# Five of seven opening groups of unread matmuls left out of a delta-rule and Fourier-mixing kernel

## The chip, the cores and the metric

One core of one Trainium2 chip. The metric is the device time of one execution in microseconds (us). 649.44 us is the median of three runs of the kernel before (649.12 to 649.47).

## The reference

The kernel joins an attention block with a recurrent state (the delta rule) and a Fourier mixing block with an MLP. There are 4 batches, 8 heads, 768 positions and 48 channels per head; the model width is 8 x 48 = 384.

```
k_n = k / (norm(k) + 1e-6)
for t in range(768):
    y[t]  = q[t] @ state
    v_old = state^T @ k_n[t]
    state = state + beta[t] * outer(k_n[t], v[t] - v_old)
x = y as (batch, seq, 384)
u = x + real(fft(fft(x, axis=seq), axis=channels))
un = layer-normalised u
out = u + relu(un @ w_ch1) @ w_ch2
```

## The kernel before

The sequence of a batch is cut into blocks of 128 positions; one batch and one block of all 8 heads is a unit, 24 units in all. Units are worked on in rounds: the first of four units, the second of two, and six of three. Within a unit, the recurrence over 64 positions is turned into matrix form, so that a small triangular matrix has to be inverted for each head; the rest are matmuls. The Fourier transforms are matmuls with tables, and the MLP is two matmuls with weights that come as 64-bit floats and are converted on the chip.

**The order of all work is planned ahead.** The class Plan (lines 74 to 394) takes operations with their dependencies, engines and estimated durations; `schedule` (line 190) simulates the engines with a list scheduler and writes down one order over all engines in `self.order`; `issue` (line 387) then walks through that order and emits the instructions, engine by engine in that order. `pace` (line 374) ties a load that SP issues after 6 us of planned time to the last computing operation that the plan has ended by then, so loads follow the computation.

**Unread matmuls.** The planner has a model of the clock of TensorE, and where TensorE would have nothing to do in some stretches, it puts in operations of its own, with the number -1 (lines 273 to 285). What they emit is in `idle` (lines 2256 to 2272). If the planned time is under E2 = 5.0 us, a group is six matmuls of 128 rows and 64 columns on the zeroed tile pb (line 2263); the profile shows two records for each, so 12 matmul records and 12 weight loads. Later groups are one or two matmuls of 256 columns (line 2270), on pb first and on the table pack later. Nobody reads their results: they go to a free PSUM bank. E0 = 1.0 us is the planned time from which groups are put in. Each group is planned as 0.432 us long at full clock.

**How the kernel opens.** SP issues the loads of k for the first six units (tile us, `load`, line 670, by `dma`, line 613, whose instructions have line 615), then q and v. ScalarE's queue loads pack (the identity and masks) and beta. VectorE and GpSimd zero tiles, pb among them. TensorE's order is: seven groups on pb (line 2263), the transposes of unit 0's k (`turn`, line 688; instructions at line 571), the transposes of beta (line 2078), two groups of line 2270, then transposes of the next unit and key products of the one before it (`keys`, line 709; instructions at line 568) in turn, up to the sixth unit. Then come 16 groups of two matmuls (line 2270, 64 records in the profile), the transposes and products of the q of the first units, and 14 groups more (56 records). VectorE and ScalarE copy each transposition out of PSUM (lines 577 and 579) and collect the key products in the tile gd (lines 577 and 748). VectorE turns gd round (line 902), inverts the small triangular matrices column by column (lines 928 to 968, tiles w and tmp) and turns the result back (line 986); TensorE's first products of the next stage read that.

```
for i in range(6):
    I(nc.tensor.matmul(pst[two[0]][0:64, 64 * i:64 * i + 64], lhsT=w[:, 0:64],
                       rhs=w[:, 64:128], start=True, stop=True,
                       skip_group_check=True))
```

Of the kernel before, what the change touches and what calls it, by code (L numbers as in the profile page):

```python
# [38 lines left out]
WIN, WARM, COLD, CLOCK = 3.413, 600.0, 560.0, True  # L39
LOOK, EARLY = 1e9, 19.0271  # L40
FOLD, BY, SEQ, HOT, HOTPE, HOTPK, HOTG, NORM = 1, 1, 1, 1.7459, 0, 0, 0, 1
HOTC, PORT, E2 = 1, 1, 5.0
GAP, HALF = 0.3228, 84.0008
LATE = -8.0806
PLOOK, PHOLD, PEND = 28.9494, 0.4978, 115.7679
# [28 lines left out]
class Plan:  # L74
# [312 lines left out]
    def issue(self):  # L387
        at = {}
        for o in self.order:
            self.ins = None  # L390
            o.fn(o.eng)
            at[id(o)] = self.ins
            if o.after is not None:
                self.tc.add_manual_dep(self.ins, at[id(o.after)].name, mybir.DependencyInfo(
                    mybir.DependencyClass.Sync, mybir.DependencyReason.DATA), reason="pace")
# [1913 lines left out]
```

## Time and profile before

| | |
|---|---|
| median of three runs | 649.44 us |
| the profiled execution | 648.84 us |
| its span, first to last instruction | 647.0 us |
| mean granted TensorE clock | 0.995 |
| instructions | 22,705 |

The profile is of one execution. Lines such as L568 are lines of the kernel; many instructions have the line of a helper (568 matmul, 571 transposition, 577 and 579 copies by ScalarE and VectorE, 615 loads). PE is TensorE's matmul and PEld its weight load, DVE is VectorE, ACT ScalarE, POOL GpSimd, SP SyncE. "out<-in" names the tiles. A row of the chain of waits has start, length and what; a row of the timeline has start, length, engine, line, operation and count, and in brackets the idle time before and who ended it. A matmul's record includes its latency, so records overlap and a busy TensorE is not one at its peak.

### The profile page before, as it was taken

The numbers are of one execution on the slowest core, as the hardware profiler recorded it, in microseconds if no ns is written. First come the engines' busy times: TensorE is split into PE (matmuls) and PEld (weight loads), VectorE is DVE, ScalarE is ACT, GpSimd is POOL, SyncE is SP. The second block draws the span as 40 slices with busy tenths as digits, with TensorE's granted clock in tenths as the row PEclk, the third lists the DMA queues.
The fourth block names the chain that finished last, engine by engine and source line by source line (L and its number), as shares of the span: only waits on it lengthen the run. The fifth ranks groups of instructions, "written<-read, shape, count | busy, mean of one in ns | idle before, by whom it ended". The sixth has DMA issues, their size and how long they took to land.

```text
span 647.0 us, 22705 instructions
## 1 busy us (share of the span) xinstructions
PE 632.9 (98%) x9748; PEld 516.6 (80%) x9748; DVE 507.3 (78%) x1529; ACT 271.6 (42%) x804; POOL 39.8 (6%) x44
## 2 busy tenths in 40 slices
PE   9998899999999999999999999999999999999998
PEld 8788788777777877877777777877777699899997
DVE  4998779999997379999863899999828633976573
ACT  3769665543154544421655333345442113321120
POOL 4103313230000000000000000000000000000000
PEclk9999889999999999999999999999999999999999
DMA  6654534550013231000323220000000000000000
GB/s 126 142 161 134 123 100 110 135 152 2 25 28 87 54 64 27 25 1 2 71 46 64 52 51 2 23 5 3 3 27 3 2 24 1 26 2 25 2 25 24
DMA packets 82808, 31.98 MB, mean 49 GB/s; under 512 B 75667, under 2 KB 79732, under 8 KB 82580
## 3 DMA queue, kind: packets, MB, share of 16 engines
q1 hardware_dynamic: 82516, 30.31, 19.3%
q8 instruction: 76, 1.25, 0.8%
q10 hardware_dynamic: 192, 0.23, 0.2%
q14 instruction: 24, 0.20, 0.1%
HBM read 25.81 MB, written 4.72 MB: 47 GB/s over the span
## 4 chain that ended last, share of the span: by engine, by line
PE 77%; DVE 15%; ACT 4%; issue 2%; DMA 1%; DVEq 0%; ACTq 0%
PE pp L568 72%; PE pp L571 3%; DVE rr L1056 2%; DVE tmp L1051 2%; PE pp L2270 1%; PE pp L2263 1%; ACT us L577 1%; DMA ws<-in_moe_w_ch_dram 1%; DVE gd L812 1%; DVE w L968 1%; ACT w L2017 1%; DVE tmp L962 1%; DVE R L1453 1%; DVE rr L902 1%; DVE w L2036 1%
## 5 line engine op out<-in xcount | busy, mean ns | idle before, releaser
L568 PE MATMUL pp<-R,w 128*128 128x256 f32 (+1 forms) x832 | 182.2, 367 | 0.7 <-DVE us L789 0.7
L568 PEld LDWEIGHTS pp<-R,w 128*128 128x128 f32 x832 | 145.6, 190 | 20.2 <-DVE us L789 0.9
L568 PE MATMUL pp<-w,R 128*128 128x384 f32 x384 | 134.6, 495 | 0.0
L577 ACT ACTIVATE us<-pp 32x128 f32<-32x128 f32 (+3 forms) x232 | 73.1, 348 | 87.4 <-PE pp L568 65.2
L568 PEld LDWEIGHTS pp<-w,R 128*128 128x128 f32 x384 | 70.2, 190 | 41.3
L1697 ACT ACTIVATE R<-pp 128x512 f32<-128x512 f32 x47 | 28.1, 597 | 102.3 <-PE pp L568 92.8
L568 PE MATMUL pp<-us 64*64 64x64 f32 (+4 forms) x2784 | 67.1, 231 | 0.0
L568 PEld LDWEIGHTS pp<-us 64*64 64x64 f32 (+2 forms) x2784 | 56.9, 132 | 5.8 <-issue 3.2
L1056 DVE TENSOR_TENSOR rr<-rr,tmp 128x84 f32<-128x84 f32 (+13 forms) x180 | 57.7, 335 | 1.5
L1051 DVE TENSOR_TENSOR tmp<-rr 128x84 f32<-128x84 f32 (+14 forms) x180 | 57.2, 332 | 1.4
L577 ACT ACTIVATE R<-pp 128x192 f32<-128x192 f32 (+8 forms) x103 | 29.7, 332 | 29.5 <-PE pp L568 18.4
L568 PEld LDWEIGHTS pp<-u,us 64*64 64x64 f32 (+2 forms) x1248 | 29.0, 129 | 15.6 <-issue 10.2
L577 ACT ACTIVATE x<-pp 64x192 f32<-64x192 f32 x91 | 28.3, 323 | 27.4 <-PE pp L568 24.0
L1362 DVE TENSOR_TENSOR u<-u,pp 64x192 f32<-64x192 f32 x66 | 22.1, 349 | 18.8 <-PE pp L568 14.5
L1391 DVE TENSOR_TENSOR st<-st,pp 128x192 f32<-128x192 f32 x30 | 10.5, 351 | 33.5 <-PE pp L568 30.4
L1872 DVE TENSOR_TENSOR us<-us,pp 128x256 f32<-128x256 f32 x64 | 26.8, 420 | 12.3 <-ACT us L577 10.8
L2270 PE MATMUL pp<-pack 64*64 64x256 f32 (+1 forms) x198 | 35.0, 396 | 0.1
L568 PE MATMUL pp<-u,us 64*64 64x48 f32 (+3 forms) x1248 | 34.5, 217 | 0.0
L568 PE MATMUL pp<-st,us 48*64 48x48 f32 (+2 forms) x1184 | 29.5, 223 | 2.6 <-issue 1.1
L568 PEld LDWEIGHTS pp<-st,us 48*64 48x64 f32 (+2 forms) x1184 | 25.0, 135 | 8.3 <-issue 4.9
L1828 DVE TENSOR_TENSOR gd<-us 128x128 f32<-128x128 f32 x48 | 11.8, 289 | 21.8 <-ACT us L1904 15.4
L568 PE MATMUL pp<-us,gd 128*128 128x192 f32 x144 | 27.8, 327 | 0.0
(176 smaller groups left out, 999.6 us busy)
## 6 DMA issues: line engine op xcount, KB each, us to landing
out_dram<-x SPq DMA_DIRECT2D x11, 384.0 KB
us<-in_k_dram SPq DMA_DIRECT2D x16, 192.0 KB
us<-in_q_dram SPq DMA_DIRECT2D x16, 192.0 KB
us<-in_v_dram SPq DMA_DIRECT2D x16, 192.0 KB
us<-in_k_dram SPq DMA_DIRECT2D x8, 181.5 KB
us<-in_q_dram SPq DMA_DIRECT2D x8, 181.5 KB
us<-in_v_dram SPq DMA_DIRECT2D x8, 181.5 KB
x<-in_moe_w_ch_dram SPq DMA_DIRECT2D x3, 484.0 KB
```

What stands on the lines that cost most here:

```text
L568: I(nc.tensor.matmul(o, lhsT=lhsT, rhs=rhs, start=start, stop=stop, skip_group_check=True))
L571: I(nc.tensor.matmul(o, lhsT=src, rhs=ident[p0:p0 + n, p0:p0 + n], is_transpose=True, start=start, stop=True, skip_group_check=True))
L577: I(nc.scalar.activation(o, i, ACT.Copy, **({} if scale is None else {"scale": scale})))
L812: I(nc.vector.scalar_tensor_tensor(w[0], w[1], (m1, m0)[s], w[2], op0=ALU.mult, op1=ALU.add))
L1051: I(eng(e).tensor_tensor(T_, R[:, :, j + 1:32, j:j + 1].broadcast_to([128, ns, n, j]), R[:, :, j:j + 1, 0:j].broadcast_to([128, ns, n, j]) ...
L1056: I(eng(e).tensor_tensor(R[:, :, j + 1:32, 0:j], R[:, :, j + 1:32, 0:j], T_, op=ALU.add))
L1362: I(nc.vector.tensor_tensor(U[:, s], U[:, s], psum(b1[s])[a, s0:s1].rearrange("p (j d) -> p j d", d=D), op=ALU.subtract))
L1391: I(nc.vector.tensor_tensor(sn[:, s0:s1], so[:, s0:s1], psum(b2)[:, s0:s1], op=ALU.add))
L1697: I(nc.scalar.activation(o, s, ACT.Relu))
L1828: vec(128, lambda e, j=j, i0=i0, i1=i1, op=op: I(nc.vector.tensor_tensor(s(j), i0, i1, op=op)), [aH] + rd, [aS(j)], pr - P.ev)
L1872: vec(256, lambda e: I(nc.vector.tensor_tensor(o, i0(), i1(), op=ALU.add)), [], [aH] + list(wr), pr - P.ev, use=n)
L2270: I(nc.tensor.matmul(pst[two[0]][x, 0:256], lhsT=w[x, 0:n], rhs=w[x, 0:256], start=True, stop=True, skip_group_check=True))
```

## The change

`issue` skips the planner's own operations whose planned start lies from 2.5 to 5.4 us. The plan is made as before and its order is the same, so all other instructions follow each other on each engine as they did. Of the seven groups of six matmuls that open TensorE's program the first two stay and the last five are gone: 30 calls, 60 matmul records and 60 weight loads.

```diff
-HOTC, PORT, E2 = 1, 1, 5.0
+HOTC, PORT, E2, E3 = 1, 1, 5.0, 2.5
...
     def issue(self):
         at = {}
         for o in self.order:
+            if o.i < 0 and E3 <= o.start < E2 + 0.4:
+                continue
             self.ins = None
             o.fn(o.eng)
```

## The prediction

> **What bounds the kernel now.** I read the page first, for the engine that carries the end and for the first chain, then the chain of waits over the first 37 us, then the instructions of TensorE in order of time, then windows and DMA at the places that the change touches.
>
> ```profile
> span 647.0 us, 22705 instructions
> ...
> PE 632.9 (98%) x9748; PEld 516.6 (80%) x9748; DVE 507.3 (78%) x1529; ACT 271.6 (42%) x804; POOL 39.8 (6%) x44
> ...
> PE 77%; DVE 15%; ACT 4%; issue 2%; DMA 1%; DVEq 0%; ACTq 0%
> ```
>
> TensorE has work in nearly all of the span, but 98% says little here: much of the early work is matmuls that nobody reads. The chain (start, length, what) tells which stretch counts:
>
> ```profile
> 1.18 7.20 PE pp L2263 x84
> 8.38 0.39 PE pp L571 x8
> ...
> 13.76 0.62 PE pp L568 x32
> ...
> 14.83 0.45 ACT gd L577
> ...
> 16.62 1.96 DVE rr L902
> ...
> 24.84 0.33 DVE us L579
> ...
> 35.90 0.98 DVE gd L986
> 36.88 0.14 issue
> 37.01 4.90 PE pp L568 x160
> ```
>
> The reader is to see three legs: 84 unread matmuls (42 calls, two records each; seven groups of 12), then the transposes and key products of six units to about 14.4, then VectorE's inversion to 36.9, where TensorE takes over. Whatever moves the first leg moves all that follows, if TensorE keeps pace beside VectorE. The second condition is in TensorE's own order of time:
>
> ```profile
> 8.31 0.46 PE L571 MATMUL pp<-pack,us 64*128 64x64 f32 x8
> 8.70 0.56 PE L2078 MATMUL pp<-pack,x 32*128 32x32 f32 x6
> 9.19 1.13 PE L2270 MATMUL pp<-pb 128*128 128x256 f32 x4
> 10.25 0.46 PE L571 MATMUL pp<-pack,us 64*128 64x64 f32 x8
> 10.64 0.69 PE L568 MATMUL pp<-us 48*64 48x64 f32 x32
> ...
> 14.71 0.70 PE L2270 MATMUL pp<-pack 128*128 128x256 f32 x2
> 15.34 1.16 PE L568 MATMUL pp<-us 48*64 48x64 f32 x64
> 16.32 7.08 PE L2270 MATMUL pp<-pack 64*64 64x256 f32 x64
> 23.33 0.96 PE L571 MATMUL pp<-pack,us 64*128 64x64 f32 x24
> ...
> 30.58 6.21 PE L2270 MATMUL pp<-pack 64*64 64x256 f32 x56
> 37.01 2.08 PE L568 MATMUL pp<-gd,w 64*64 64x64 f32 x64 [0.22 <-DVE gd L986]
> ```
>
> Two more runs of unread matmuls (L2270, 7.0 and 6.2 us) stand in TensorE's order and block it while they last; the second ends at 36.79, only 0.22 us before VectorE's result. So at 37 us **two chains arrive together**, VectorE's and TensorE's, and TensorE has a slack of 0.22 us.
>
> **What the change removes.** Five groups of 12: 60 matmuls and their 60 weight loads. Their price is not one number, because the pace changes inside the stretch:
>
> ```profile
> 1.18:5.80 4.62, 4.62 (x43) 1.00 0.94 193
> 5.80:8.40 2.60, 2.60 (x46) 1.00 1.05 208
> ```
>
> Columns: window, length, PE busy (instructions), granted clock, DMA. The same instruction is issued each 4.62/43 = 0.107 us up to 5.8, and then the other 41 in 2.51 us, each 0.061 us. The clock cell says 1.00 in both, so it can't be trusted here: I read the pace as a slow clock up to 5.8. The two groups kept are 24 x 0.107 = 2.57 us and end at 1.18 + 2.57 = 3.75. The five removed are 19 at 0.107 and 41 at 0.061, 4.5 us.
>
> **What is late next.** TensorE's first read instruction needs the pack table and the first k load. Packets that had gone by 3.55 and by 4.3 us:
>
> ```profile
> q1 hardware_dynamic: 1035, 0.20, 27.2%
> ...
> q1 hardware_dynamic: 1965, 0.37, 42.6%
> ```
>
> A k load is 8 heads x 128 rows = 1024 lines of 192 bytes. If the loads go in order, the first is in by 3.6; if two share the engines, by 4.3; and the semaphore instruction ahead of the transposes bounds it from above:
>
> ```profile
> L571 PEldq EVENT_SEMAPHORE  x1: 51/51/51, 7.2 to 7.2; - x1
> ```
>
> It passes at 7.2, whether it had to wait or only stood in the queue. I take **4.35**: the packets are nearer to that than to 7.2. At 930 packets in 0.75 us the other units follow each 0.8 us, earlier than TensorE asks for them. The transposes then start 8.31 - 4.35 = 3.96 us earlier. That is the most that can be won. No wait is added, but this one becomes visible, with all of TensorE's order behind it.
>
> SP's loads from 12 us on go along with it, since they wait for what was computed, so a shift does not meet a fixed DMA time:
>
> ```profile
> SPq L615 <- ACT us L577: 5.2, 4, 1.5
> SPq L615 <- DVE us L579: 5.2, 1, 5.2
> ```
>
> **What the five groups did for the clock.** This is the term that decides. The only other place where the trace shows the clock go down and up again (same columns, with PEld, DVE, ACT and POOL between):
>
> ```profile
> 67.25:70.67 3.42, 2.83 (x59) 2.25 (x57) 3.33 (x9) 2.81 (x10) 0.00 (x0) 1.00 0.56 111
> 70.67:74.08 3.41, 3.41 (x98) 3.12 (x96) 2.08 (x7) 2.38 (x8) 2.61 (x2) 1.00 0.69 167
> 74.08:77.49 3.41, 1.80 (x66) 1.54 (x64) 3.33 (x9) 1.41 (x4) 0.21 (x1) 1.00 0.71 207
> 77.49:80.91 3.42, 3.42 (x59) 3.15 (x58) 1.72 (x5) 2.15 (x6) 3.42 (x2) 0.50 0.37 70
> 80.91:84.32 3.41, 3.41 (x31) 2.60 (x28) 0.65 (x2) 2.08 (x7) 0.49 (x1) 0.50 0.47 93
> ```
>
> The clock is set in steps of 3.41 us. It fell after a step with 1.80 us of work, and one whole step with TensorE busy for 3.42 of 3.42 did not bring it back: only the second did. The records include their latency, so by streaming time (the columns of each matmul at 0.107 us for 64) I make the failing step about 94% (some 0.2 us between its shapes) and the one that worked 95% or more. Before the change the groups fill one step without a gap (2.40 to 5.81, on the same grid of 3.41 us), and the clock came at 5.8. After it the groups fill 2.57 us, then come 0.6 us of nothing, then transposes and products with a change of shape each half a microsecond. One unit's pair (L571 x8, L568 x32) takes 1.02 us, of which 12 issues x 0.061 are 0.73: 0.145 us goes at each change. So the best step there is filled to about 88%. I take it that **the clock stays low** until a long run fills a step: the 64 L2270 matmuls.
>
> [...]
>
> **The sum with a low clock.** A row gives four 64-row products of 128 columns:
>
> ```profile
> 78.02 1.98 PE L568 MATMUL pp<-us 48*64 48x128 f32 x32
> 79.78 0.95 PE L568 MATMUL pp<-st,us 64*64 64x64 f32 x13
> ```
>
> 1.76 us for 8 fours, so 0.11 us for a four of 64 columns. Then, with 0.145 us for each change:
> - a transposition: 4 pairs x 0.107 + 0.145 = 0.57 (0.39 before); a key product: 8 x 0.11 + 0.145 = 1.02 (0.63 before); the pair 1.6 instead of 1.02;
> - L2078: between 0.49 (as now) and 0.98 (doubled); I take 0.75;
> - the four L2270: 1.06 now, of which some 0.2 for changes; the rest doubled, 1.9.
>
> From 4.35: 4.92, 5.67, 7.57 after the first transposition, L2078 and L2270; then 0.57 + 1.02 for the first two, and three pairs: 9.16 + 4.8 = 13.96 for the fourth unit's product, which ended at 14.38. VectorE's chain starts **0.4 us earlier**. TensorE goes on: a transposition 0.57, two L2270 1.06, 16 fours 1.9: 17.5 instead of 16.32, **1.2 us later**. Now the 64 L2270 start at the low clock, 0.22 instead of 0.11 us each. A step must lie wholly in them or the fours just before (from 15.6 to 17.5), and where the steps lie in another execution is open, so the clock comes between 19.0 and 24.3; I take the middle, 21.6. The run ends at 21.6 + 7.0 - (21.6 - 17.5)/2 = 26.55, where it ended at 23.33: 3.2 us later (1.9 to 4.6).
>
> From there TensorE's work up to 36.79 is the same at full clock. VectorE has a copy of those late transposes in its order (L579 at 24.84), so it loses its 0.4 us there and waits some 2 us too. At 37.01 the end is TensorE's: 3.2 - 0.22 = 3.0 later. One stall of TensorE's weight loads lies between, and may take part of it back:
>
> ```profile
> PEld pp L568 <- issue: 0.6, 1, 0.6
> ```
>
> With 0.5 of that I take **+2.5 us**, with ends +1.2 and +4.0. After 37 us each stage waits for the one before it and all keep the shift.
>
> **Code loading** I cost at nothing, with both ends open:
>
> ```profile
> PEld pp L568 <- issue: 21.8, 54, 1.2
> ...
> q8 instruction: 76, 1.25, 0.8%
> ```
>
> 76 loads for 2 x 9748 instructions are one for each 256; 120 fewer moves each by half a block. The 54 stalls that may be theirs have a mean of 0.4 us and a longest of 1.2, so a shift could give or take about 1 us.
>
> The profiled execution took 648.84 us (span 647.0 and 1.84 around it), 0.60 below the median 649.44. 648.84 + 2.5 = 651.34; with 0.60 put back, **651.9 us**. A measurement of this kernel tells about 0.2% (1.3 us) from no change.
>
> **Rivals.**
> - **Early clock** (the other side, faster). The point that decides: does one step with TensorE busy to about 88% lift the clock? For it: the groups' step did with one. Against it: the step at 77.49. It would come between 7.8 and 11.2, say 9.5, after the first product; the other three pairs run at 1.02 us and the fourth product ends at about 12.4 instead of 14.38. TensorE and VectorE are both 2.0 us earlier (1.4 to 2.5): 647.4. The ceiling, if the clock were high from 4.35 on, is 3.96 us: 645.5.
> - **Clock after two busy steps**, as at 77.49. It comes near 12.6; the fourth product ends near 13.5, TensorE's leg 0.7 earlier: -0.8, 648.6, within what can be told from no change.
> - **Not what it says**: the first k load is later than I read, near 7.2, and TensorE waits in place of the groups. Then up to 1.1 us are won at the start and the clock lost all the same: between 649 and 653.
>
> **Chances.** Low clock into the long run 0.52 (0.49 of it above +1.3 us); early clock 0.27; two steps 0.13 (0.03 of it below -1.3); the rest, late load or code loading, 0.08, spread over all. Faster by over 0.2%: 0.27 + 0.03 + 0.03 = 0.33; slower: 0.49 + 0.02 = 0.51; within: 0.16. The likeliest case alone spans 650.6 to 653.5. The range takes in most of the early clock: **647.0 to 653.5**.
>
> **What would show it.** TensorE's L2263 row: x24 from 1.18, ending near 3.75. L571's first start: 4.3 to 4.4 if the first load is as read; later means the load. L571 and L568 between 5 and 14 us: pairs each 1.6 us are a low clock, 1.02 a high one. The first run of 64 L2270: an end at 25 to 28 bears me out, one before 22 the early clock. VectorE's L902: near 16.2. L568 on gd at 37.01: 39 to 40 against 35. I am wrong if that last row starts before 37, or if it is late and the end of the span is not.

## The result and the profile after

The kernel after takes **653.08 us** (median of 20 runs, 648.98 to 660.51), the one before 649.23 us on the same chips (20 runs, 647.12 to 652.01). Medians in this document are of all runs; the ratios leave out a run more than 1.5% above its kernel's fastest (660.51 here, and one run each of e1_refill and e9_tab_pieces). The ratio after to before is **1.0063**, with a 95% interval of 1.0042 to 1.0084: 4.1 us slower (2.7 to 5.5). The forecast was 651.9 us in 647.0 to 653.5. Lines of the kernel after are two higher: L570 is what L568 was, L573 was L571, L2265 was L2263, L2272 was L2270.

The page of the kernel after (its profiled execution took 653.18 us):

```profile
span 651.4 us, 22585 instructions
...
PE 632.7 (97%) x9688; PEld 514.5 (79%) x9688; DVE 507.4 (78%) x1529; ACT 271.6 (42%) x804; POOL 39.8 (6%) x44
...
PE 81%; DVE 13%; ACT 3%; issue 3%; DMA 1%; DVEq 0%; ACTq 0%
```

The 60 matmuls are gone (9748 to 9688), and the span is 4.4 us longer. The opening is not where this comes from. TensorE in order of time:

```profile
1.18 2.82 PE L2265 MATMUL pp<-pb 128*64 128x64 f32 x24 [1.18 <-DVE pb L695]
...
4.12 0.46 PE L573 MATMUL pp<-pack,us 64*128 64x64 f32 x8
...
6.06 0.46 PE L573 MATMUL pp<-pack,us 64*128 64x64 f32 x8
...
7.08 0.46 PE L573 MATMUL pp<-pack,us 64*128 64x64 f32 x8
...
32.83 2.08 PE L570 MATMUL pp<-gd,w 64*64 64x64 f32 x64 [0.21 <-DVE gd L988]
```

The transposes start at 4.12 where they started at 8.31; the next two are 1.02 us apart, the pace of a high clock; and the products on gd start at 32.83 instead of 37.01. In this execution the opening gained 4.2 us. An instruction that runs 30 times between 196 and 503 us, VectorE's update of the state, is a ruler for the rest (count, shortest/median/longest ns, first and last start). First before, then after:

```profile
L1391 DVE TENSOR_TENSOR st<-st,pp x30: 333/354/355, 196.5 to 503.0; 128x192 f32<-128x192 f32 x30
```

```profile
L1393 DVE TENSOR_TENSOR st<-st,pp x30: 340/354/355, 196.6 to 507.3; 128x192 f32<-128x192 f32 x30
```

Of the 4.2 us won by 37 us nothing is left at 196 (+0.1), and 4.2 more are lost by 507. The chain of waits shows the first loss:

```profile
42.73 4.36 PE pp L570 x171
47.10 1.79 issue
48.89 2.80 PE pp L570 x91
...
52.88 2.48 issue
55.36 7.74 PE pp L570 x179
```

TensorE stands still twice, for 1.79 and 2.48 us, with no engine that releases it. The window from one restart up to the next stall (columns as in the prediction):

```profile
48.88:52.95 4.07, 3.99 (x128) 3.56 (x128) 2.89 (x9) 3.37 (x12) 0.15 (x1) 1.00 0.81 291
```

128 matmuls and 128 weight loads stand between the two stalls: 256 instructions, the size that the prediction had worked out for one load of code. The queue that loads code moved nothing from 51.75 to 53, then one block of code between 53.0 and 54.2, and TensorE started again at 55.36, 1.2 us after that window. The row of the code queue in it (packets, MB, share):

```profile
q8 instruction: 1, 0.02, 5.0%
```

TensorE's idle times by who ended them (sum, count, longest), before and after:

```profile
PE pp L568 <- issue: 1.5, 2, 1.1
```

```profile
PE pp L570 <- issue: 7.1, 5, 2.5
...
PEld pp L570 <- issue: 29.6, 63, 2.6
```

The weight loads' longest was 1.2 us before. Behind two of the three long stalls the granted clock is 0.50 for a step of 3.41 us. Around the third, 1.66 us that end at 214.86, two steps of the clock in the kernel after, with the step behind the second stall as a third row, and then the same stretch as the first two before the change:

```profile
212.17:215.59 3.42, 1.76 (x81) 1.47 (x68) 0.70 (x2) 1.61 (x6) 0.00 (x0) 1.00 0.30 58
215.59:219.00 3.41, 3.41 (x7) 1.74 (x6) 0.00 (x0) 1.43 (x6) 0.00 (x0) 0.50 0.04 7
...
55.16:58.58 3.42, 3.22 (x48) 2.88 (x48) 1.07 (x5) 1.58 (x5) 3.40 (x3) 0.50 0.02 5
```

```profile
212.10:215.51 3.41, 3.41 (x89) 2.49 (x76) 0.70 (x2) 3.06 (x11) 0.00 (x0) 1.00 0.33 65
215.51:218.92 3.41, 3.41 (x149) 2.74 (x148) 2.07 (x7) 1.28 (x5) 0.00 (x0) 1.00 0.34 67
```

After the step with 1.76 us of work the granted clock is 0.50 for the next one, as it is behind the stall that ends at 55.36; before the change it stays at 1.00 around 215. The price can be read off the eight matmuls that follow (pp<-w,R, 384 columns): 4.54 us instead of 2.85. With the 1.66 us of the stall that is 3.35 of the 4.2 us lost between the ruler's ends.

### The profile page after: what moved, and what is told of

It reads as the page before. It is cut to its first block, busy times and chain, and to the rows that moved or that the text cites. A ratio compares the mean times of both kernels' runs of the same rounds, so it can differ in the third digit from the quotient of the medians.

```text
span 651.4 us, 22585 instructions
## 1 busy us (share of the span) xinstructions
PE 632.7 (97%) x9688; PEld 514.5 (79%) x9688; DVE 507.4 (78%) x1529; ACT 271.6 (42%) x804; POOL 39.8 (6%) x44
## 4 chain that ended last, share of the span: by engine, by line
PE 81%; DVE 13%; ACT 3%; issue 3%; DMA 1%; DVEq 0%; ACTq 0%
PE pp L570 75%; PE pp L573 3%; DVE rr L1058 2%; DVE tmp L1053 2%; PE pp L2272 2%; DMA us<-in_q_dram 1%; DVE gd L814 1%; DVE w L970 1%; DVE tmp L964 1%; DVE rr L904 1%; ACT x L579 1%; DVE rr L860 0%; ACT us L579 0%; PE pp L2265 0%; ACT w L2019 0%
## 5 line engine op out<-in xcount | busy, mean ns | idle before, releaser
L570 PE MATMUL pp<-R,w 128*128 128x256 f32 (+1 forms) x832 | 183.9, 370 | 0.7 <-DVE us L791 0.7
L570 PEld LDWEIGHTS pp<-R,w 128*128 128x128 f32 x832 | 146.8, 192 | 20.8 <-DVE us L791 0.9
L570 PE MATMUL pp<-w,R 128*128 128x384 f32 x384 | 136.3, 500 | 0.0
L570 PEld LDWEIGHTS pp<-w,R 128*128 128x128 f32 x384 | 70.9, 192 | 42.2 <-issue 1.7
L570 PE MATMUL pp<-us 64*64 64x64 f32 (+4 forms) x2784 | 67.5, 230 | 6.4 <-issue 6.4
L570 PEld LDWEIGHTS pp<-us 64*64 64x64 f32 (+2 forms) x2784 | 56.9, 132 | 12.6 <-issue 10.1
L570 PEld LDWEIGHTS pp<-u,us 64*64 64x64 f32 (+2 forms) x1248 | 29.6, 130 | 15.7 <-issue 10.2
L570 PE MATMUL pp<-u,us 64*64 64x48 f32 (+3 forms) x1248 | 35.3, 219 | 0.0
L2272 PE MATMUL pp<-pack 64*64 64x256 f32 (+1 forms) x198 | 34.8, 395 | 0.1
L570 PE MATMUL pp<-st,us 48*64 48x48 f32 (+2 forms) x1184 | 29.0, 222 | 1.8 <-DVE st L1393 0.7
L570 PEld LDWEIGHTS pp<-st,us 48*64 48x64 f32 (+2 forms) x1184 | 24.4, 134 | 7.6 <-issue 3.7
L570 PE MATMUL pp<-us,gd 128*128 128x192 f32 x144 | 27.8, 327 | 0.0
```

The source lines that it names most:

```text
L570: I(nc.tensor.matmul(o, lhsT=lhsT, rhs=rhs, start=start, stop=stop, skip_group_check=True))
L2272: I(nc.tensor.matmul(pst[two[0]][x, 0:256], lhsT=w[x, 0:n], rhs=w[x, 0:256], start=True, stop=True, skip_group_check=True))
```

## Theories and experiments

**Theory A**: TensorE's code is loaded in blocks of 256 instructions (an estimate: 2 x 9748 instructions for the 76 loads of the kernel before) that end at fixed counts of its stream. Leaving out 120 instructions moves every block end onto other work, and where the new ends fall into short matmuls the load comes too late. **Theory B**, the forecast: in most executions the clock stays low in the opening, and that is the loss. **Theory C**, formed after the first three runs: executions come in two kinds, by whether the groups kept lift the clock at once or not.

### Put the instructions back without work: e1_refill

On the kernel after, the unread matmuls of the first long run are issued in halves, so that 120 instructions come back with no more columns. The block ends beyond 26 us lie on the same work as before the change.

```diff
-                I(nc.tensor.matmul(pst[two[0]][x, 0:256], lhsT=w[x, 0:n], rhs=w[x, 0:256],
+                for c in ((0, 128), (128, 256)) if mode == "64" and 13.5 < now < 20.0 else ((0, 256),):
+                    I(nc.tensor.matmul(pst[two[0]][x, c[0]:c[1]], lhsT=w[x, 0:n], rhs=w[x, c[0]:c[1]],
```

> The changed kernel with 120 instructions put back later: 15 of the 16 groups in the first long run of unread matmuls (L2270 in the kernel before) are issued as halves of 128 columns, so that TensorE streams the same columns in the same time but its code blocks of 256 instructions end from there on where they ended before the change. Theory A (the code blocks have moved, and their late loads stop TensorE behind 40 us): the 4 us won in the opening stay, 645 to 647 us, and the stalls of 2.0 and 2.7 us near 47 and 53 us are gone. Theory B (low clock in the opening of most executions, as forecast): no better than the changed kernel, 652 to 654.

646.23 us against 649.22, ratio 0.9969 (0.9944 to 0.9995). The ruler and the waits:

```profile
L1393 DVE TENSOR_TENSOR st<-st,pp x30: 327/353/355, 193.1 to 499.3; 128x192 f32<-128x192 f32 x30
```

```profile
PE pp L570 <- issue: 0.8, 1, 0.8
...
PEld pp L570 <- issue: 21.1, 53, 1.0
```

The opening's gain is now kept to the end (-3.4 at 193, -3.7 at 499), and the long stalls are gone. So with its block ends put back the same removal is not slower but **faster**, though its interval only just excludes no change: A. The intervals of this kernel and of the kernel after (1.0042 to 1.0084) lie well apart.

### Move the block ends alone: e2_shift_only

On the kernel before, the seven opening groups do the same columns in 12 matmuls instead of 42: 120 instructions fewer, meant to take TensorE the same time.

```diff
-                for i in range(6):
-                    I(nc.tensor.matmul(pst[two[0]][0:64, 64 * i:64 * i + 64], lhsT=w[:, 0:64],
-                                       rhs=w[:, 64:128], start=True, stop=True,
+                for i in range(2 if now < 4.4 else 1):
+                    m = 256 if now < 4.8 else 128
+                    I(nc.tensor.matmul(pst[two[0]][0:64, 0:m], lhsT=w[:, 0:64],
+                                       rhs=w[:, 0:m], start=True, stop=True,
```

> The kernel before with its seven opening groups issued as 12 matmuls of up to 256 columns in place of 42 of 64: TensorE streams unread columns up to about 8.4 us as before, but with 120 instructions fewer, so the code blocks stand as in the changed kernel. Theory A: the loss without the gain, stalls of 2 us and more near 51 and 57 us, 653 to 658. Theory B: as before, 649 to 650.

653.92 us against 649.22, ratio 1.0082 (1.0054 to 1.0109). TensorE in order of time, and the ruler:

```profile
1.18 8.14 PE L2264 MATMUL pp<-pb 128*64 128x256 f32 x24 [1.18 <-DVE pb L693]
9.26 0.46 PE L571 MATMUL pp<-pack,us 64*128 64x64 f32 x8
...
54.28 0.40 PE L568 MATMUL pp<-us 64*64 64x64 f32 x12 [2.04 <-issue]
```

```profile
L1391 DVE TENSOR_TENSOR st<-st,pp x30: 335/353/356, 198.1 to 509.7; 128x192 f32<-128x192 f32 x30
```

It is not a pure shift: the transposes start 0.95 us late (9.26 against 8.31). Beyond that, the stall stands before the same 12 matmuls as in the kernel after, and from 198 to 510 us it loses 5.1 us (+1.6, then +6.7). Counted in the traces, 1113 matmuls start before the restart at 54.28, and 1113 before the one at 48.89 in the kernel after; the later stalls, too, stand at the same counts in both (3661, 5824 and 7988). In the kernel before, where the count 1113 falls on other work, TensorE waits 0.35 us there.

### The change once more: e3_again

The kernel after, unaltered, for another execution's profile.

> The changed kernel once more, for a second look at its opening. Theory A: first products of the next stage (tile gd, 37.01 us before) near 33 us in this execution too, stalls at 47 and 53 us, 652 to 654. Theory B: the clock comes later than 8 us and those products start after 37 us.

653.63 us against 649.22, ratio 1.0082 (1.0054 to 1.011). This profiled execution (656.88 us) opened in the other way:

```profile
4.23 0.69 PE L573 MATMUL pp<-pack,us 64*128 64x64 f32 x8 [0.23 <-DMA us<-in_k_dram]
...
7.64 0.69 PE L573 MATMUL pp<-pack,us 64*128 64x64 f32 x8
...
9.31 0.69 PE L573 MATMUL pp<-pack,us 64*128 64x64 f32 x8
...
17.89 8.28 PE L2272 MATMUL pp<-pack 64*64 64x256 f32 x64
...
39.39 2.08 PE L570 MATMUL pp<-gd,w 64*64 64x64 f32 x64
```

A transposition takes 0.69 us instead of 0.46, a pair 1.67 instead of 1.02. The run of 64 takes 8.28 instead of 7.08 us, so some 11 of its matmuls ran at the low clock (1.20 us at 0.11 each), and the clock came about 2.4 us into it, at 20.3. The products on gd start 2.4 us late. This is the forecast's opening, and it shows what didn't lift the clock here: three steps in a row with TensorE busy throughout in the records (the last three rows). The first row shows where the steps lie here: one ends at 3.24, behind 19 of the 24 matmuls kept.

```profile
3.24:6.66 3.42, 3.19 (x25) 2.67 (x24) 1.01 (x18) 0.38 (x1) 3.42 (x4) 1.00 1.12 230
6.66:10.07 3.41, 3.41 (x55) 2.41 (x57) 0.90 (x5) 0.39 (x1) 1.74 (x3) 1.00 0.72 144
10.07:13.48 3.41, 3.41 (x88) 2.94 (x92) 0.83 (x3) 1.46 (x4) 0.00 (x0) 1.00 0.29 58
13.48:16.90 3.42, 3.42 (x70) 2.54 (x71) 2.74 (x7) 2.83 (x10) 0.00 (x0) 1.00 0.37 76
```

(The clock column reads 1.00 here as in the prediction's windows; the pace tells.) The ruler shows another loss on top of it, +3.2 at 200 us and +8.0 at 511:

```profile
L1393 DVE TENSOR_TENSOR st<-st,pp x30: 339/354/356, 199.7 to 511.0; 128x192 f32<-128x192 f32 x30
```

```profile
PE pp L570 <- issue: 3.3, 3, 1.4
```

One thing that A had expected is missing: the stalls of 1.8 and 2.5 us at 47 and 53 us aren't in this execution. Its three stalls stand at the later counts, 3661, 5824 and 7988, the longest with 1.39 us; why the two earlier block ends cost no stall here isn't shown.

So B's opening holds too, in this execution: the same program opens 4.2 us early or 2.4 us late. That is C.

### More groups kept, block ends put back: e4_three and e5_four

Three and four groups are kept, and 12 and 9 groups of the long run halved, so that all block ends beyond lie as before.

```diff
-HOTC, PORT, E2, E3 = 1, 1, 5.0, 2.5
+HOTC, PORT, E2, E3 = 1, 1, 5.0, 3.0
```

> As e1_refill, but three of the seven opening groups stay and 96 instructions are put back (12 groups in halves), so the code blocks end where they did before the change. The groups end near 5.0 us. Theory C (e1_refill has two kinds of executions, by whether the two groups lift the clock): the opening is 3.2 us earlier than before where the clock comes, and more executions are of that kind than with two groups: 646 us, few over 649. If the spread of e1_refill had another cause, the spread stays as it was and the median is about 647.

> As e4_three with four groups kept and 72 instructions put back (9 groups in halves). The groups end near 6.2 us, 2.1 earlier than before. Theory C: nearly all executions get the clock by then, 647 us, with a spread like that of the kernel before. Otherwise the spread of e1_refill.

Three: 646.77 against 649.14, ratio 0.9965 (0.9947 to 0.9983). Four (E3 = 3.8): 646.90, ratio 0.997 (0.9952 to 0.9987). Both profiled executions opened at the high clock. They don't differ from e1_refill by more than the intervals, and theirs lie clearer of no change; the runs of four lie between 643.07 and 648.95, where those of e1_refill go up to 654.07.

### The other way: e6_other_way

The kernel before with the halves of e1_refill: nothing is left out, 120 instructions are added, and the block ends beyond 23 us move the other way.

> The kernel before, all seven groups kept, with 15 groups of the first long run of L2270 in halves: 120 instructions more, so the code blocks move by as much the other way, with the same streaming time. Theory A in its general form (the order was planned round the places where the blocks end): slower than before, 651 to 655. Theory A in its narrow form (only the late load behind the table's load near 53 us costs): 649 to 650 unless such a load falls on dense work there too.

654.96 against 649.14, ratio 1.0088 (1.0065 to 1.0112). TensorE in order of time, the window between two stalls, and the ruler:

```profile
53.06 0.28 PE L568 MATMUL pp<-us 64*64 64x64 f32 x4 [1.55 <-issue]
...
58.98 0.45 PE L568 MATMUL pp<-us 64*64 64x64 f32 x11 [1.93 <-issue]
```

```profile
53.05:58.97 5.92, 3.99 (x128) 3.56 (x128) 4.99 (x11) 5.30 (x17) 1.35 (x1) 1.00 0.57 203
```

```profile
L1391 DVE TENSOR_TENSOR st<-st,pp x30: 336/353/356, 195.6 to 507.1; 128x192 f32<-128x192 f32 x30
```

Again 128 and 128 between two stalls, and 5.0 us lost between the ends of the ruler (-0.9, then +4.1). The restarts stand at the counts 1241 and 1369, 128 and 256 matmuls behind 1113. It is the same stretch of work for a plain reason: with an end every 256 instructions, 120 more and 120 fewer put the ends only 16 instructions apart, here 8 matmuls later in the work. So this run confirms e2_shift_only by another edit, and is not a second place of the ends: these ends make a kernel with all seven opening groups 0.9% slower.

### No group at all: e8_none

All seven groups are left out, and 21 groups of the later runs halved, which gives back all 168 instructions.

```diff
-HOTC, PORT, E2, E3 = 1, 1, 5.0, 2.5
+HOTC, PORT, E2, E3 = 1, 1, 5.0, 0.0
```

> All seven opening groups are left out and 168 instructions put back (16 groups of the first long run and 5 of the second in halves), so the code blocks end where they did. TensorE's first instruction is then the transposes at about 4.2 us at the low clock. Theory C: the clock comes only in the long run of L2270, near 20 us, in every execution, as in the low-clock opening of e3_again, and TensorE is 2 to 3 us late at 37 us: 651 to 653, one kind of executions. Without Theory C: 645 to 647.

650.72 against 649.14, ratio 1.0017 (0.9995 to 1.004).

```profile
4.23 0.69 PE L573 MATMUL pp<-pack,us 64*128 64x64 f32 x8 [4.23 <-DMA us<-in_k_dram]
...
39.06 2.08 PE L570 MATMUL pp<-gd,w 64*64 64x64 f32 x64
```

Without the groups the transposes start no earlier than in the kernel after, since k's load ends their wait, and the products on gd start 2.0 us late. Eight of 12 runs lie between 650.45 and 653.98, four between 647.5 and 648.7. C had expected one kind, at 651 to 653; the four were not profiled and are unexplained.

### The big table in pieces: e9_tab_pieces

Ahead of the second stall's late load a table of 1155 KB, issued at 48.07, was on its way: from 48.8 to 53 us q1 moved 1.18 MB, and the code queue nothing. Here its load is four loads of a quarter of the columns each.

```diff
-    dma(tab, cn["tab"].ap().rearrange("p t c -> p (t c)"), [A(tab, 0, 1)], 0, kb=1180)
...
+        for i in range(4):
+            c0, c1 = n * i // 4, n * (i + 1) // 4
+            I(nc.sync.dma_start(out=tab[:, c0:c1], in_=src[:, c0:c1]))
```

> The changed kernel with one edit: the load of the Fourier table (tab, 1155 KB, lines of 9240 bytes), beside which TensorE's next code block came late near 53 us, is issued as four pieces with lines of 2310 bytes. If the block waits behind long lines of that load (theory A1), it comes 1 to 3 us sooner, the stall of 2.7 us near 53 us shrinks under 1, and the kernel takes 651 to 652. If the block is late because 256 instructions last TensorE less time than a load of code takes, whatever else is loaded (theory A2), the stall stays and the time is that of the changed kernel, 653 to 654.

652.36 against 648.6, ratio 1.0047 (1.0024 to 1.007): not apart from the kernel after. Its profile has no stall at 47 or 53 us, but it opened in yet another way, with the clock up near 9 us, between the two kinds above, so TensorE met the block ends at other times. But e3_again, with the table in one load, has no stall at those two ends either. **Inconclusive** on whether the table's load delays the code. From the ruler's first to its last update (195.0 to 507.7) it loses 6.2 us beside the kernel before, so later stalls remain (three idle times of TensorE without a releaser, the longest 1.4 us).

### A plan that knows: e10_plan_knows

The planner counts no instructions for the skipped groups. For Plan has a model of code loading of its own: it counts TensorE's instructions in blocks of 256, 24 for each opening group, and lengthens an operation that runs past a block's end before the planned arrival of the next (`fetch`, line 159). So the order of the kernel before was planned for its own block ends.

```diff
+                        if E3 <= now < E2 + 0.4:
+                            best.ni = 0
```

> The changed kernel, but the planner counts no instructions for the five groups that are left out, so it plans with the block ends where they now are; the plan's order changes in many places with it. Theory A: the loss to the blocks goes, 645 to 650, if the new order is otherwise as good as the old, which nothing promises; theory B (opening alone): 653.

662.77 against 648.6, ratio 1.0206 (1.0183 to 1.0229). The plan writes another order for the whole kernel, and a stall of 2.4 us is in it too, where A had expected 645 to 650. Order and block ends change together, so this says only that planning anew was no remedy.

### Block ends halfway: e11_half_refill

The kernel after with 8 groups halved: 64 of 120 instructions back, so the block ends lie 56 instructions from where they were.

> The changed kernel with 64 of the 120 instructions put back (8 groups of the first long run in halves): the block ends stand 56 instructions away from where they were instead of 120. Theory A: a time of its own between 645 and 655 according to what work those ends meet, and stalls of TensorE that the trace puts at block ends; no smooth way from 653 to 646 is expected. Theory B: 653.

646.93 against 648.6, ratio 0.9974 (0.9944 to 1.0004). The longest code stall of the weight loads is 0.5 us, where the kernel after has 2.6:

```profile
PEld pp L570 <- issue: 20.1, 53, 0.5
```

So the ends needn't lie exactly where they did. The runs fall into two groups: seven at 644.04 to 647.2, five at 650.6 to 652.65. The profiled one is of the second group, and shows why:

```profile
39.34 2.08 PE L570 MATMUL pp<-gd,w 64*64 64x64 f32 x64
```

### Both together: e12_four_half

Four groups kept (E3 = 3.8) and two halved: block ends as in e11_half_refill.

> Four opening groups as in e5_four, and the block ends where e11_half_refill has them, 56 instructions from the old place (2 groups of the first long run in halves put 16 of the 72 back). Theory A and C together: TensorE waits for code as little as in e11_half_refill and nearly all executions get the clock in the opening, 644 to 647 us with a spread of some 4 us. If the blocks of e11_half_refill were no better than the old ones: as e5_four, 646.9.

**645.25** against 649.25, ratio **0.9939** (0.9916 to 0.9962), faster than both kernels.

```profile
1.18 5.32 PE L2265 MATMUL pp<-pb 128*64 128x64 f32 x48 [1.18 <-DVE pb L695]
6.43 0.46 PE L573 MATMUL pp<-pack,us 64*128 64x64 f32 x8
...
35.15 2.08 PE L570 MATMUL pp<-gd,w 64*64 64x64 f32 x64 [0.16 <-DVE gd L988]
```

```profile
L1393 DVE TENSOR_TENSOR st<-st,pp x30: 335/353/355, 193.2 to 499.2; 128x192 f32<-128x192 f32 x30
```

The transposes start 1.9 us early and so do the products on gd (35.15 against 37.01); at the ruler's ends it is 3.3 and 3.8 us ahead, so it also wins some 1.4 us between 37 and 193 that the opening doesn't explain. Its eight runs lie between 642.32 and 646.77, in one group.

## Why the prediction came out

The number was right by luck, and the reason mostly was not: the forecast gave the whole loss to the opening, and the runs give it to the code. An opening put at +2.5 us measured -2.0, code loading put at nothing measured +5.3, and the two errors nearly cancel. Each term by itself:

| what | runs | ratio | us |
|---|---|---|---|
| opening alone, over both kinds of executions (after, block ends put back) | e1_refill | 0.9969 | -2.0 (-3.6 to -0.3) |
| block ends alone, 120 fewer | e2_shift_only | 1.0082 | +5.3 (3.5 to 7.1) |
| block ends alone, 120 more | e6_other_way | 1.0088 | +5.7 (4.2 to 7.3) |
| both | after | 1.0063 | +4.1 (2.7 to 5.5) |

The us are the ratio times 649.2. The first two sum to +3.3, within the interval of the measured +4.1. Of e2's +5.3 up to about 1 may be its later transposes.

- **The groups kept, right.** 24 matmuls from 1.18; their row ends at 4.00 where 3.75 was forecast, the 0.31 us of its last record included; the next transposes start at 4.12.
- **The first k load at 4.35, right within 0.2**: 4.12 in the kernel after; in e3_again and e8_none the load itself ends TensorE's wait, at 4.23.
- **"The clock stays low", true for one kind of execution.** There the steps hold well: pairs 1.67 (1.6 forecast), the run of 64 at 17.89 (17.5), its end at 26.2 (26.55), the clock at 20.3 (19.0 to 24.3), the products on gd 2.4 late (+2.5). In e11_half_refill, which opened that way and has no long stalls, +3.0 and +1.7 us are left at the ruler's ends. But other executions, the profiled one of the kernel after among them, opened at the high clock and 4.2 us early. That is the rival "early clock" with a better price: not 2.0 us but the ceiling of 3.96, as the clock was up before the first transposition and not at 9.5. It did not come by the mechanism as priced, a step of transposes and products: in e3_again three such steps in a row didn't lift the clock. The step that failed here is where the steps lie. The forecast laid them as in the kernel before, with an end at 2.40 that cuts the two groups. In the kernel after and in e1_refill all 24 matmuls fall into one step (0.55 to 3.96 and 0.67 to 4.09), and the clock was up behind it; in e3_again and e11_half_refill a step ends at 3.24 and 3.15, behind 19 and 18 of them, and it stayed low. That is a match in four executions, not a test.
- **Code loading "at nothing, with about 1 us either way", the step that failed.** The count of one load per 256 instructions was right (128 matmuls and 128 weight loads between two stalls, twice), and so was "moves each by half a block". The size was not: +5.3 us for 120 fewer and +5.7 for 120 more, two shifts that put the ends at nearly the same place; a shift of 56 cost nothing that shows (e11_half_refill). At most block ends little shows, even after: 76 loads, and five idle times of TensorE's matmuls without a releaser, 7.1 us in all. But the bound was read from the stalls of the kernel before, whose longest was 1.2 us, and those say what its own block ends cost, and nothing of ends that fall elsewhere. After the shift some fall into stretches of short matmuls (256 instructions in 4.07 us between the first two stalls), and stalls of 1.7 to 2.5 us come, two of the three with a halved clock behind them. The kernel's source gave a sign: its order was planned with the block ends in mind (see e10_plan_knows), and the change takes instructions out after the plan is made.
- **"After 37 us each stage keeps the shift", right only where block ends are as before or near**: from the first to the last update of the ruler the shift changes by -1.3 to +0.8 us in e1, e4, e5, e8, e11 and e12, and by +4.2 to +6.2 in the kernel after, e2, e3, e6 and e9.
- **The last test of the forecast named the case wrongly.** "I am wrong if that last row starts before 37": it did, at 32.83, and the kernel was slower all the same.

What stays open: what exactly lifts the clock. The first whole step of the kernel after, whose pace was high right behind it, and that of e2_shift_only, where it was not:

```profile
0.55:3.96 3.41, 2.78 (x24) 2.63 (x24) 1.97 (x14) 1.49 (x2) 3.23 (x5) 1.00 0.68 150
```

```profile
0.38:3.79 3.41, 2.61 (x6) 1.45 (x7) 1.97 (x14) 1.49 (x2) 3.12 (x7) 1.00 0.61 142
```

About the same time, 2.78 and 2.61 us, is covered by 24 matmuls in the one and by 6 in the other. Whether the count matters, the weight loads, or the 0.17 us between them, wasn't told apart. Nor was what delays a late code load told apart: TensorE's own pace or the table's load ahead of it. And that the two groups of runs in e1_refill and e11_half_refill are the two openings rests on one profiled execution of each.

## What to carry to other kernels

Leaving 120 instructions out of TensorE's stream brought its code stalls onto other work here: at the count 1113 it waits 1.79 and 2.04 us in the two kernels without them (after, e2_shift_only), 0.35 before. Before such an edit is judged, give back the count with work that costs little (here matmuls in halves: the first long run took 7.20 us instead of 7.08), or the edit and the shift are measured as one. Here the same removal was 0.6% slower without that and 0.3% faster with it. A bound for code loading read from a kernel's own stalls need not hold for a shifted kernel (1.2 us at the longest before, 2.6 after): look for stretches where 256 instructions last only a few us (4.07 here). Not every shift hurts: 56 instructions cost nothing that shows, and a shift in the other direction can end at nearly the same place, as 120 more and 120 fewer did.

## What the runs showed of the hardware

- Two stalls exactly 128 matmuls and 128 weight loads apart, in two kernels whose block ends lie 16 instructions apart in the work (48.88 to 52.95 after, 53.05 to 58.97 in e6_other_way), and stalls at the same counts of matmuls (1113, 3661, 5824, 7988) in two kernels with different openings (after, e2_shift_only). In the kernel after, the restart at 55.36 came some 1.2 us behind a stretch in which the block had arrived.
- A step of 3.42 us with 1.76 us of work, broken by a 1.66 us stall, was followed by a step at a granted clock of 0.50, in which eight matmuls took 4.54 us instead of 2.85: that code stall cost twice.
- The opening clock differs between executions of one program: up by 4.1 us in one (eight transposes in 0.46 us from there on), at 20.3 in another (0.69 until then), some 6.6 us apart at 33 to 39 us, 1% of the kernel.
